# A shift filter moved from 64-channel to 32-channel diagonal blocks, in a fused convolution and token-mixing kernel

## The chip, the cores and the metric

One core of a Trainium2 chip runs the whole kernel. The metric is the device time of one execution in microseconds. Three executions before the change took 174.65, 175.32 and 174.4 us; the median is 174.65 us. The engines are named as in the profile: PE (TensorE matmul), PEld (its weight loads), DVE (VectorE), ACT (ScalarE), POOL (GpSimd) and SP (SyncE, which here only issues DMAs).

## The reference, cut to what matters

Sequence length S is 2048, channels D 448, hidden size F 1792, all in bf16.

```python
def _A_ref(q, k, v, shift_k, ssm_k, ssm_D):
    k_pad = jnp.pad(k, ((0, 0), (ks - 1, 0), (0, 0)))
    k_shift = jnp.zeros_like(k)
    for t in range(ks):                       # ks = 4
        k_shift = k_shift + k_pad[:, t:t + S, :] * shift_k[:, ks - 1 - t][None, None, :]
    kv = k_shift * v
    # y = causal convolution over S of kv with ssm_k, one filter per channel (by FFT of length 2 S)
    y = y + kv * ssm_D[None, None, :]
    return q * y

def _B_ref(x, w1, b1, w2, b2):
    h = _layernorm(x, axis=-1)
    u = _gelu(jnp.einsum("bsd,sf->bdf", h, w1) + b1)
    return (jnp.einsum("bdf,fs->bds", u, w2) + b2).transpose(0, 2, 1)

x = A_q
h = x + _A_ref(_layernorm(x, axis=-1), A_k, A_v, A_shift_k, A_ssm_k, A_ssm_D)
h2 = h + _B_ref(_layernorm(h, axis=-1), B_w1, B_b1, B_w2, B_b2)
```

The change touches the first part: the four-tap shift filter on k, its product with v, and the load of the long filter ssm_k (448 channels by 2048 positions).

## The kernel before, in words

Sequence position s is held as s = 16 q + r: q is the partition (128) and r (16 values) lies along the free axis. All SBUF tiles are views of one tensor, which the profile calls `arena`; all PSUM is `ps`, with eight banks. The stages are these, with the lines that the profile names.

- **Loads** (SP queue). The filter ssm_k comes as four chunks of channels, 128, 128, 128 and 64 (L877), the last one into 64 partitions of 4096 bytes. k comes in four pieces of four r each (L888), and so does v (L891). Small tables are the shift taps (L880, L883), ssm_D (L895) and the biases (L898, L900).
- **kT**. The filter chunks are transposed on PE (L1028) so that positions lie on partitions; DVE copies them out of PSUM (L731). Nine filler matmuls, whose result nobody reads (L1015), stand ahead of everything, and three more behind each of the first three chunks.
- **kv**. k is transposed on PE (L956) and copied out, so that channels lie on partitions. The shift filter is then a matmul with the transposed k as weights and, as the moving operand, diagonal matrices `DG` (built by DVE at L941 from an identity and the taps): a column block for each tap. A weight load holds 64 channels, so two of them, on two row tiles of 64, stand in the array side by side (L982). The work has eight units: four groups of four r, times two pairs of channel chunks. A unit fills two PSUM banks. DVE multiplies what it finds there by v and writes over v (L997, two a unit).
- **Stage 1** of the transform, for the filter ("k1") and for kv ("u1"): matmuls on four column tiles of 32 (L1049), copied out by ACT or DVE (L1059, and L1057 where ssm_D is added), and reordered across partitions by DMAs within SBUF (L1065: two on the POOL queue, one on SP, for each half group).
- **Stage 2** ("k2", "u2"): L1084, copied out by L728, L729, L731 and L732.
- **Products and first inverse stage** ("i1"): DVE products (L1150), matmuls (L1167), copies (L728), DMAs within SBUF (L1190, L1179).
- **Second inverse stage and layernorm** ("i2"): L1289 and L1297, then a chain over DVE, ACT and POOL to the normalised rows (L1375).
- **MLP**: L1422 (first seven blocks of F), L1432 (the other seven), L1444 (the second product), L1447 (residual) and the stores.

Nothing of this order is written as a loop that runs on the chip. The program hands every operation to a planner, with an estimated cost, the buffers that it reads and writes, and a due time. The due time is looked up in the table `WHEN`, by stage and step; a smaller number goes first. The planner simulates the five engines, starts on each the ready operation with the smallest number, and writes the instructions in that order, with the waits that they need. PSUM banks are given out in that simulation, singly or in pairs. Operations that may run on ACT or DVE are given to one of them by the table `WHERE` (a: ACT, d: DVE, f: whichever the planner finds free). So each engine's order is fixed when the program is built, and an instruction that waits holds back all that stand behind it on its engine.

The stage-1 matmuls read whole rows of 448 channels, so "k1" needs all four filter chunks, and "u1" needs all channels of its rows of kv.

## Time and profile before

| What | Number |
|---|---|
| median of three executions | 174.65 us |
| span of the profiled execution, first to last instruction | 173.7 us |
| PE busy | 161.4 us (93%), 1419 matmuls |
| DVE busy | 103.1 us (59%) |
| ACT busy | 89.7 us (52%) |
| POOL busy | 58.8 us (34%) |
| granted TensorE clock | 1.000 |

The median lies 0.95 us above the span of the profiled execution. The span has five stretches. Up to about 11 us the inputs arrive. From 11 to 41 us PE is busy nearly without a gap on the transposes, the shift filter and stage 1. From 41 to 73.5 us ACT and DVE are. From 73.5 to 77 us the last reorder is awaited. From 77 us to the end PE works without a gap through the second inverse stage and the MLP, 94 us of it. So what happens ahead of 77 us moves the end by as much as it moves the start of that last stretch.

### The profile page before, as it was taken

The numbers are of one execution on the slowest core, as the hardware profiler recorded it, in microseconds if no ns is written. First come the engines' busy times: TensorE is split into PE (matmuls) and PEld (weight loads), VectorE is DVE, ScalarE is ACT, GpSimd is POOL, SyncE is SP. The second block draws the span as 40 slices with busy tenths as digits, with TensorE's granted clock in tenths as the row PEclk, the third lists the DMA queues.
The fourth block names the chain that finished last, engine by engine and source line by source line (L and its number), as shares of the span: only waits on it lengthen the run. The fifth ranks groups of instructions, "written<-read, shape, count | busy, mean of one in ns | idle before, by whom it ended". The sixth has DMA issues, their size and how long they took to land.

```text
span 173.7 us, 3570 instructions
## 1 busy us (share of the span) xinstructions
PE 161.4 (93%) x1419; PEld 92.1 (53%) x1419; DVE 103.1 (59%) x191; ACT 89.7 (52%) x129; POOL 58.8 (34%) x152
## 2 busy tenths in 40 slices
PE   6989999979989999838999999999999999999994
PEld 2766745442333332424345555555567777777783
DVE  7997899868979999979897751000002132231231
ACT  3796757798999999878883455421120000000000
POOL 8345717680912524564989640000000000000000
PEclk9999999999999999999999999999999999999999
DMA  5999865783859668755999999930000111101111
GB/s 163 408 299 380 284 177 213 301 330 117 244 113 389 198 193 258 246 168 166 392 396 402 416 423 421 417 150 0 0 0 4 53 53 53 44 9 57 53 53 53
DMA packets 15628, 35.15 MB, mean 202 GB/s; under 512 B 3740, under 2 KB 9740, under 8 KB 15612
## 3 DMA queue, kind: packets, MB, share of 16 engines
q1 hardware_dynamic: 12468, 28.25, 44.7%
q0 software_dynamic: 2880, 6.49, 11.4%
q8 instruction: 11, 0.18, 0.4%
q10 hardware_dynamic: 264, 0.18, 0.3%
q14 instruction: 5, 0.04, 0.1%
HBM read 22.05 MB, written 1.84 MB: 137 GB/s over the span
## 4 chain that ended last, share of the span: by engine, by line
PE 61%; DVE 11%; DMA 10%; ACT 8%; POOL 5%; issue 2%; SPq 1%; DVEq 0%; ACTq 0%; POOLq 0%
PE ps L1444 24%; PE ps L1432 12%; PE ps L1422 9%; DMA arena<-arena 6%; DVE arena L1150 5%; DMA arena<-in_A_ssm_k_dram 5%; ACT arena L1059 4%; PE ps L1084 3%; ACT arena L728 3%; PE ps L1049 3%; PE ps L982 2%; PE ps L1167 2%; PE ps L1028 2%; DVE arena L1226 2%; ACT arena L729 2%
## 5 line engine op out<-in xcount | busy, mean ns | idle before, releaser
L1447 DVE SCALAR_TENSOR_TENSOR arena<-ps,arena 128x448 bf16<-128x448 f32 (+2 forms) x17 | 11.1, 656 | 55.7 <-PE ps L1444 55.7
L1444 PE MATMUL ps<-arena 128*128 128x448 bf16 (+2 forms) x238 | 42.7, 342 | 0.0
L1444 PEld LDWEIGHTS ps<-arena 128*128 128x128 bf16 x238 | 33.3, 145 | 9.5
L728 ACT CAST arena<-ps 128x896 bf16<-128x896 f32 (+1 forms) x31 | 24.9, 943 | 1.1 <-PE ps L925 0.6
L1422 PE MATMUL ps<-arena 128*128 128x448 bf16 x112 | 23.1, 353 | 0.9 <-DVE arena L1364 0.6
L1059 ACT CAST arena<-ps 128x896 bf16<-128x896 f32 x23 | 19.5, 913 | 6.6 <-PE ps L1049 6.5
L1065 POOL DMA_DIRECT2D arena<-arena x32 | 17.5, 553 | 13.3 <-ACT arena L1059 12.6
L1432 PE MATMUL ps<-arena 128*128 128x448 bf16 x112 | 21.7, 352 | 0.0
L1084 PE MATMUL ps<-arena 128*64 128x448 bf16 x128 | 16.0, 361 | 1.8 <-ACT arena L1059 0.9
L1412 ACT ACTIVATE arena<-ps,arena 128x448 bf16<-128x448 f32 x14 | 8.2, 640 | 17.5 <-PE ps L1432 15.1
L1150 DVE TENSOR_TENSOR arena<-arena 128x1792 bf16<-128x1792 bf16 x16 | 16.6, 1081 | 0.9 <-DMA arena<-arena 0.9
L1422 PEld LDWEIGHTS ps<-arena 128*128 128x128 bf16 x112 | 10.5, 98 | 12.2 <-DVE arena L1375 3.0
L1432 PEld LDWEIGHTS ps<-arena 128*128 128x128 bf16 x112 | 11.0, 98 | 10.2
L1167 PE MATMUL ps<-arena 64*128 64x448 bf16 x128 | 14.3, 351 | 1.8 <-DVE arena L1150 0.8
L1049 PE MATMUL ps<-arena 128*32 128x448 bf16 x256 | 15.1, 355 | 0.6 <-DVE arena L997 0.3
L1190 POOL DMA_DIRECT2D arena<-arena x14 | 8.2, 589 | 16.4 <-ACT arena L728 16.4
L1344 ACT ACTIVATE arena<-arena 128x448 bf16<-128x448 f32 x14 | 8.1, 575 | 7.1 <-DVE arena L1316 6.9
L1084 PEld LDWEIGHTS ps<-arena 128*64 128x64 f16 x128 | 5.4, 108 | 11.4 <-ACT arena L728 3.8
L1167 PEld LDWEIGHTS ps<-arena 64*128 64x128 f16 x128 | 5.0, 94 | 10.9 <-ACT arena L728 5.3
L1289 PE MATMUL ps<-arena 128*128 128x448 bf16 x32 | 7.7, 353 | 2.6 <-DMA arena<-arena 2.6
L731 DVE COPY arena<-ps 128x1024 bf16<-128x1024 bf16 (+2 forms) x15 | 9.2, 648 | 0.6 <-PE ps L1028 0.6
L1049 PEld LDWEIGHTS ps<-arena 128*32 128x32 f16 x256 | 5.0, 95 | 8.4 <-DVE arena L997 2.6
(96 smaller groups left out, 190.3 us busy)
## 6 DMA issues: line engine op xcount, KB each, us to landing
arena<-in_B_w_dram SPq DMA_DIRECT2D x8, 896.0 KB, 10.3
arena<-in_B_w_dram SPq DMA_DIRECT2D x2, 2048.0 KB, 17.5
arena<-arena SPq DMA_DIRECT2D x16, 224.0 KB, 3.4
arena<-arena POOLq DMA_DIRECT2D x32, 112.0 KB, 3.4
arena<-in_B_w_dram SPq DMA_DIRECT2D x2, 1536.0 KB, 18.9
arena<-arena POOLq DMA_DIRECT2D x14, 196.0 KB, 4.2
arena<-in_A_k_dram SPq DMA_DIRECT2D x4, 448.0 KB, 6.0
arena<-in_A_v_dram SPq DMA_DIRECT2D x4, 448.0 KB, 9.2
```

The costliest lines, as they stand in the source:

```text
L728: return e.copy(out=dst(), in_=src())
L731: return e.tensor_copy(out=dst(), in_=src())
L1049: op("pe", lambda e, W, b=b, r=r, q=q, x=x, c0=c0: e.matmul(PS[32 * q:32 * q + 32, b.slots[x], 0:D], E[:, 2 * r + x, c0:c0 + 32], src[:, r ...
L1059: return e.copy(out=dst, in_=Ppair(b)) if W == "act" else e.tensor_copy(out=dst, in_=Ppair(b))
L1065: shuf[tag].append(op(q_, lambda e, W, g=g, i=i, a=a, nu=nu, jh=jh: e.dma_start(T[a + i:a + i + 4 * nu - 3:4].rearrange("p (j k) c d -> p ...
L1084: op("pe", lambda e, W, b=bs[h], h=h, j=j, c=c, par=par: e.matmul(PS[64 * par:64 * par + 64, b.slots[c], 0:D], FW[:, 64 * c:64 * c + 64], ...
L1150: op("dve", lambda e, W, m=m, i=i: e.tensor_tensor(out=MR(m.slots[0]).rearrange("p (x y) d -> p x y d", x=2), in0=TU[:, i].unsqueeze(2).br ...
L1167: k = op("pe", lambda e, W, b=bs[h], m=ms[h], par=par, t=t, tab=tab, xy=xy, P=P: e.matmul(Pb(b, par), tab[P, :], MR(m.slots[0])[P, xy, :], ...
L1422: op("pe", lambda e, W, r=r, fc=fc, b=bs[fc]: e.matmul(Pb(b), W1A[:, r, 128 * fc:128 * fc + 128], Q[:, r, :], start=(r == 0), stop=(r == R ...
L1432: op("pe", lambda e, W, r=r, fc=fc, b=b: e.matmul(Pb(b), W1B[:, r, 128 * (fc - n0):128 * (fc - n0) + 128], Q[:, r, :], start=(r == 0), sto ...
L1444: op("pe", lambda e, W, r=r, fc=fc, b=b, d0=d0, d1=d1: e.matmul(Pb(b)[:, d0:d1], W2[fc // 7][:, fc % 7, r:S:R], G[:, fc, d0:d1], start=(fc ...
L1447: op("dve", lambda e, W, r=r, b=b, A=A, d0=d0, d1=d1: e.scalar_tensor_tensor(out=X[:, r, d0:d1], in0=Pb(b)[:, d0:d1], scalar=bm[:, r:r + 1 ...
```

## The change

Four things are changed, and the order of all instructions with them.

1. The diagonal blocks have 32 channels instead of 64. Four weight loads, on four row tiles of 32 partitions, stand in the array side by side. The units are now seven: groups of eight r for each of the three full chunks (six units), and one for the last chunk, whose two copies on the two halves of the partitions serve r 0 to 7 and r 8 to 15. A unit has 11 source rows times 4 tiles, 44 matmuls, and fills two pairs of PSUM banks, 256 columns in each bank. DVE multiplies each pair by v, 14 products of 512 elements in all. `DG` has half the columns; one small addition more builds the folded identity.
2. The filter's last chunk is loaded into all 128 partitions, with the first 1024 positions in the lower half and the others in the upper half. Its 16 transposes become 32 small ones, two for each r.
3. Behind the filter chunks one filler is left instead of nine.
4. `WHEN` and `WHERE` have new values throughout, and the planner has two new constants for DMAs.

```diff
-    "loads": (106, 111, 114, 115, 217, 195, 86, 237, 90, 235, 158, 197, 227, 143, 150,),
+    "loads": (7, 10, 12, 14, 24, 20, 2, 32, 3, 30, 19, 22, 28, 11, 16,),
...
-                        fab = s + o.nbytes / o.rate
+                        fab = s + max(190.0, o.nbytes / o.rate)
...
-        N_WZ, N_WI, N_W0, N_WK, N_WJ = 2, 0, 9, 3, 0
+        N_WZ, N_WI, N_W0, N_WK, N_WJ = 2, 0, 9, 1, 0
...
-            for i, c in enumerate((0, 1, 2, 3)):
-                sch.t0 = -20.0 + i
-                op(Dq, lambda e, W, c=c: e.dma_start(KN[0:CW[c], c, :], A_ssm_k[128 * c:128 * c + CW[c], :]),
-                   w=[(o_KN + 4096 * c, 4096)], dmab=CW[c] * 4096, rate=217.0 if c == 3 else None)
+            for c in range(3):
+                sch.t0 = -20.0 + c
+                op(Dq, lambda e, W, c=c: e.dma_start(KN[:, c, :], A_ssm_k[128 * c:128 * c + 128, :]),
+                   w=[(o_KN + 4096 * c, 4096)], dmab=128 * 4096)
+            sch.t0 = -17.0
+            op(Dq, lambda e, W: e.dma_start(
+                KN[:, 3, 0:S // 2],
+                A_ssm_k[384:448, :].rearrange("c (h s) -> h c s", h=2)),
+               w=[(o_KN + 4096 * 3, 2048)], dmab=128 * 2048)
...
-                out=DG.rearrange("p c j d -> p (c j) d"), in0=I2.unsqueeze(1).broadcast_to([128, 16, 64]),
-                in1=wsc.unsqueeze(2).broadcast_to([128, 16, 64]), op=ALU.mult),
+                out=DG.rearrange("p c j d -> p (c j) d"), in0=I2[:, 0:32].unsqueeze(1).broadcast_to([128, 16, 32]),
+                in1=wsc.unsqueeze(2).broadcast_to([128, 16, 32]), op=ALU.mult),
...
+            for u, (g, c) in enumerate(((0, 0), (0, 1), (0, 2), (0, 3), (1, 0), (1, 1), (1, 2))):
+                one = c == 3
+                bs = [_Buf(psum, 2) for _ in range(2)]
+                for m, d in enumerate((0, 4, -3, -2, -1, 1, 2, 3, 5, 6, 7)):
+                    for t in range(4):
+                        base = 8 * (t // 2) if one else 8 * g
+                        i0 = max(0, d)
+                        i1 = min(7, d + 3)
+                        P = slice(32 * t, 32 * t + 32)
+                        b = bs[t // 2]
+                        op("pe", lambda e, W, b=b, c=c, t=t, d=d, i0=i0, i1=i1, rs=rs, sh=sh, P=P, m=m: e.matmul(
+                            PS[:, b.slots[t % 2], 32 * i0:32 * i1 + 32], KX[c >> 1][P, c & 1, rs, sh:sh + 128],
+                            DG[P, c, i0 - d:i1 - d + 1, :].rearrange("p j d -> p (j d)"),
+                            start=(m == 0), stop=(m == 10), skip_group_check=True),
+                           r=[(o_KX[c >> 1] + 272 * (16 * (c & 1) + rs), 272), (o_DG, 1024)], bw=[b], n=32 * (i1 - i0 + 1),
+                           est=max(7.0, 3.4 * (i1 - i0 + 1)), mode=6)
...
-                if i < 3:
+                if i < 1:
                     dummy(N_WK, T_KT + 1.0 * (2 * i + 1), (k,))
...
-                           dmab=4 * nu * 4 * DB, keng=nu, rate=350.0))
+                           dmab=4 * nu * 4 * DB, keng=nu, rate=300.0))
```

## The prediction

> **What bounds the kernel now.** I read the page first: PE's row of slices, and the chain of work that ended last. From 77 us to the end PE has no gap, so the change can move the end only by what it moves ahead of that. The chain in order of time, the page's slices and PE's timeline then show the front.
>
> ```profile
> 2.58 8.13 DMA arena<-in_A_ssm_k_dram
> 10.76 0.96 PE ps L1028 x12
> 19.71 3.28 PE ps L982 x104
> PE   6989999979989999838999999999999999999994
> GB/s 163 408 299 380 284 177 213 301 330 117 244 113 389 198 193 258 246 168 166 392 396 402 416 423 421 417 150 0 0 0 4 53 53 53 44 9 57 53 53 53
> 1.38 3.45 PE L1015 MATMUL ps<-arena 128*128 128x448 bf16 x9 [1.38 <-DVE arena L1007]
> 10.76 0.96 PE L1028 MATMUL ps<-arena 128*128 128x128 bf16 x12 [0.62 <-DMA arena<-in_A_ssm_k_dram]
> 12.03 1.18 PE L1028 MATMUL ps<-arena 64*128 64x64 bf16 x16
> ```
>
> The chain begins with a load of the filter ssm_k: it, not PE, sets when the filter's transposes (L1028) and so its stage 1 (L1049, first at 14.00 us) begin. The second of the 40 slices (4.3 us each) moves 408 GB/s, so the loads run back to back. Then the windows, by stretch (PE, weight loads, DVE, ACT, POOL), the shift filter's own share, DVE's products, and the queues:
>
> ```profile
> 19.60:41.00 21.40, 20.03 (x404) 10.59 (x400) 18.75 (x27) 15.91 (x19) 12.00 (x23) 1.00 0.73 261
> 50.00:73.50 23.50, 21.11 (x194) 7.89 (x191) 23.12 (x36) 23.12 (x29) 8.60 (x17) 1.00 0.75 241
> 19.60:41.00 21.40, 7.16 (x208) 6.27 (x208) 1.00 0.73 261
> L997 DVE TENSOR_TENSOR arena<-ps,arena 128x512 bf16<-128x512 f32 x12 | 7.8, 684 | 0.8 <-PE ps L982 0.8
> q10 hardware_dynamic: 264, 0.18, 0.3%
> ```
>
> Between 19.6 and 41 us PE is busy 94%, but DVE 88% and ACT 74%: PE bounds, DVE stands close behind. Between 50 and 73.5 us DVE and ACT are both full.
>
> **The change part by part.** The shift filter on PE goes from 208 matmuls and 7.16 us to 7 x 44 = 308. In the trace the two row tiles of a pair start 3 to 4 ns apart, and pairs follow each other 28, 57, 82 and 110 ns apart for 64, 128, 192 and 256 columns: about 2 ns and 0.42 ns a column. A new unit has eleven sets of four tiles: five of 128 columns, two each of 96, 64 and 32, so 5 x 56 + 2 x (42 + 28 + 15) = 450 ns. Seven are 3.15 us, and with a turn of 0.02 us between units 3.3 us: 3.9 us saved. If four tiles ran only as two pairs, it would be 6.3 us and 0.9 saved; under 3 us the columns exclude.
>
> How much of it arrives: with the filter shorter, DVE is next. Its products were 12 x 0.684 + 4 x 0.414 = 9.9 us and are 14 x 0.684 = 9.6; the copies of stage 1 are still there. DVE and ACT together have 18.75 + 15.91 - 0.3 = 34.4 us, or 17.2 each if the planner shares them evenly. DVE worked at 88% in this stretch, so 17.2 / 0.88 = 19.5 us instead of 21.4: 1.9 gained. If the shares stay uneven, 18.45 / 0.88 = 21.0: 0.4. At best all 3.9 arrive. I take 1.9, the even sharing, since ACT has the room.
>
> Coarser units: the first rows of kv needed two units, four products (2.2 us of DVE); they now need four units, eight products, 8 x 0.6 = 4.8 us. So "u1" can start 2.6 us later. That is covered by the filter's stage 1, half of L1049's 256 matmuls (32 took 1.70 us, so 6.7 us), which needs no kv; without that cover it costs all 2.6. A unit also holds four of the eight PSUM banks where it held two. I take 0.5, between 0 and 2.6, nearer the covered end.
>
> The load of the last chunk. Before, it is 64 rows of 4096 bytes, issued at 3.2 us and landed 8.5 us later, at 11.7. After, the memory side is written half, channel, position: its outermost count is 2, though the SBUF side counts 128. What an outermost count does is to be seen on queue 10, which carries two DMAs alone: one of 112 rows of 896 bytes into an outer count of 8 partitions, one of 128 rows over 128. Those are 240 packets; the page has 264, and the 24 others, 4 bytes each in the packet records, are one completion for each engine used: 8 and 16. So a DMA with a side of outer count 8 ran on 8 engines, and one with a side of count 2 would run on 2. Each gets 64 pieces of 2048 bytes. Packets of 4096 bytes took 159 ns and of 3584 bytes 140 ns, so 2048 take some 82 ns: 5.2 us on these two engines, where it was 4 x 159 = 0.64. (By the page, 408 / 16 = 25.5 GB/s an engine: 131072 bytes in 5.1 us.) Ahead of it each engine has two pieces of k, 2 x 8 x 140, and three chunks, 3 x 8 x 159 ns: 6.1 us, from the first packets at 2.9. So the chunk ends at 14.2 and lands, with the 0.6 us that the first chunk took beyond its last packet, at 14.8: 3.1 later. If all 16 engines carry it, it lands up to 0.4 earlier; at worst it is the full 4.6 later.
>
> [...]
>
> Its consumers: "k1" reads whole rows, so it waits for this chunk. Before, 2.3 us went by from landing to 14.00 (16 transposes at 62 ns apart, two copies). After, 32 half-size ones, between 0.5 us if the halves overlap and 2.0 us if not; I take 1.0, half of it ahead of the first copy (0.42 us) and two hops of 0.1 us. So "k1" begins near 16.3: 2.3 us later, between 1.2 earlier (16 engines: 11.3 + 0.5 + 0.42 + 0.2, and 0.4 of other transposes, 12.8) and 3.9 later (16.3 + 1.0 + 0.42 + 0.2). All loads behind it on SP's queue end behind it on those two engines: the rest of k, the taps, and v, whose last piece moves from 19.7 to about 22.2 us. That is no more than the shift of "k1", so nothing else waits on top.
>
> Of the nine fillers behind the chunks eight go. Six of the nine (0.73 us each three) lay in the wait for the load: nothing. Three (0.54 and 0.36) stood on the chain, 0.7 us; with the load late they too would have lain in a wait, so nothing, and -0.7 if it is not late. `DG` at L941 falls from 1.22 us to about 0.65, and an addition like L939's 0.18 is added; PE is at transposes then, so nothing; without that cover -0.4. ssm_D's load is issued ahead of the third chunk, and its 0.57 us on SP delays two issues; the engines are busy with earlier chunks until 8.3, so nothing, else +0.6. The planner's constants only reorder.
>
> The new order from 41 to 73.5 us: DVE and ACT are full at 23.12 of 23.5, so it can gain 0.4; at the 88% of the stretch before it would lose 2.8. I take 0, since the work is the same. From 77 us on PE has the same matmuls without a gap: 0, and it loses what it waits for if an order fails there.
>
> Sum on the profiled execution: 173.7 + 2.3 - 1.9 + 0.5 = 174.6 us. The median stands 0.95 above that span, so 175.6 us.
>
> **The rivals.** (1) PE's saving arrives in full (3.9 instead of 1.9) and the coarser units cost nothing: 175.6 - 2.0 - 0.5 = 173.1 us, faster. It decides from the point where ACT takes over a third of what DVE copies. For it: ACT idles 5.5 of 21.4 us; against it: DVE is at 88% and alone can multiply by v. (2) The load runs on all 16 engines, as the program's planner assumes: "k1" is 1.2 earlier instead of 2.3 later, 175.6 - 3.5 = 172.1 us. For it: 128 partitions on the SBUF side; against it: the outer count of 2. (3) PE's clock falls in the wait: third chunk at about 10.7, fourth at 14.8, with one filler left, is 4 us with little work. The first nine fillers took 3.45 / 9 = 383 ns each, the later ones 190, so PE starts at half speed for some 4.6 us. Were the stage behind the wait run so for as long as those nine, 3.45 us, half of it, 1.7 us, would be lost: 177.3 us. Against it: waits of 0.62 and 2.6 us did not slow it. [...] (4) The new order leaves ACT and DVE gaps from 41 to 73.5 us as before it: up to 2.8, about 178 us.
>
> **How the numbers follow.** Load on two engines and the saving half eaten: 0.42, at 175.6, of its own 174.3 to 176.9. (1) 0.22, (2) 0.14, (3) 0.15, (4) 0.07. About 0.5% (0.87 us) is what a measurement of this kernel can tell from no change. Slower by more (over 175.5): half of the first case, 0.22, and (3) and (4), 0.44. Within: most of the rest of the first case, 0.16, and a quarter of (1), 0.22 in all. Faster: 0.34. The range from 171.7 to 177.6 leaves out the lower third of (2) and the upper ends of (3) and (4), together under 0.2.
>
> **What would show it.** Right: the last chunk lands near 15 us, with 2 completions; stage 1 begins near 16.3 us; the 308 matmuls take some 3.3 us; DVE has the fewest gaps from 20 to 41 us; the last stretch is 94 us again. Wrong: a landing near 11.5 us, filter matmuls over 5 us, PE gaps behind the products, or matmuls at half speed after 15 us.

## The result, and the profile after

| | before | after |
|---|---|---|
| median of the executions shown | 174.99 us | 187.69 us (186.17 to 189.07) |
| ratio, 95% interval | | 1.067 (1.057 to 1.077) |
| span of the profiled execution | 173.7 us | 184.8 us |
| granted TensorE clock | 1.000 | 0.972 |

The change makes the kernel 12.7 us slower. The direction of the forecast held; its size, 175.6 us, did not, and the time lies far above the range. On the profiled execution the forecast had 174.6 us and 184.8 were measured: 10.2 us are to be explained.

The lines of the page that answer to those shown of before are these: PE's slices, the granted clock, the group of the products and the queue with the two small DMAs.

```profile
PE   7935998989988998874998999999999999999994
PEclk9995799999999999998899999999999999999999
q10 hardware_dynamic: 264, 0.18, 0.3%
L1000 DVE TENSOR_TENSOR arena<-ps,arena 128x512 bf16<-128x512 f32 x14 | 9.6, 691 | 3.6 <-PE ps L986 2.1
```

The clock has two dents that before did not have, in the fourth and fifth slice and around the twentieth. The products take 9.6 us, as forecast. In the chain of waits (start, duration, what), the load of the filter that heads it is now a piece of 12.19 us, where it was 8.13, and the half-size transposes follow it:

```profile
3.68 12.19 DMA arena<-in_A_ssm_k_dram
15.91 2.13 PE ps L1032 x16
```

PE's timeline (start, duration, line, tile, form, count, and the idle time before it with what ended it) shows the two waits and what runs at half speed behind them (the last line is of before):

```profile
8.15 2.76 PE L1032 MATMUL ps<-arena 128*128 128x128 bf16 x35
15.91 2.13 PE L1032 MATMUL ps<-arena 64*64 64x64 bf16 x32 [5.00 <-DMA arena<-in_A_ssm_k_dram]
18.22 2.48 PE L963 MATMUL ps<-arena 128*128 128x128 bf16 x23
20.63 0.78 PE L1055 MATMUL ps<-arena 128*32 128x448 bf16 x8
85.79 0.79 PE L1295 MATMUL ps<-arena 128*128 128x448 bf16 x2 [3.78 <-DMA arena<-arena]
86.37 1.70 PE L1303 MATMUL ps<-arena 128*128 128x448 bf16 x4
76.98 0.55 PE L1289 MATMUL ps<-arena 128*128 128x448 bf16 x2 [2.63 <-DMA arena<-arena]
```

Stage 1 (L1055) begins at 20.63 us and the second inverse stage (L1295) at 85.79. The four matmuls of L1303 behind it took 0.92 us before. The trace's record of the granted clock has two falls to half: at 14.29 us for 6.83 us, and at 85.97 us for 3.41. The windows by stretch (PE, weight loads, DVE, ACT, POOL, clock) and the shift filter's own share (L986, PE and weight loads) are:

```profile
14.00:19.60 5.60, 3.69 (x46) 3.44 (x46) 1.14 (x3) 1.18 (x2) 0.00 (x0) 0.53 0.66 233
19.60:41.00 21.40, 19.54 (x477) 10.74 (x476) 16.03 (x22) 14.75 (x17) 10.19 (x19) 0.96 0.52 177
50.00:73.50 23.50, 21.01 (x204) 7.79 (x192) 22.49 (x28) 21.77 (x27) 10.72 (x20) 1.00 0.71 221
25.00:34.50 9.50, 5.43 (x220) 4.71 (x220) 1.00 0.70 223
39.00:42.50 3.50, 2.15 (x88) 1.93 (x88) 1.00 0.92 356
```

The filter takes 5.43 + 2.15 = 7.58 us of PE, where it took 7.16 and the forecast had 3.3. These two are busy times, in which every piece of matmuls also has the length of its last one; the forecast added up distances between starts. From first start to last in each piece, the records sum to 6.21 us before (5 pieces) and 6.14 after (8 pieces). How it runs is seen on one half of a unit, 22 matmuls of two tiles in 0.64 us, 0.46 from the first start to the last:

```profile
33.33 0.64 PE L986 MATMUL ps<-arena 32*128 32x128 bf16 x22
```

From 14 to 19.6 us DVE, ACT and POOL stand nearly still. Where the 11.1 us of the profiled executions come from is read from the first instruction of each stage:

| first instruction of | before | after | later by |
|---|---|---|---|
| stage 1 | 14.00 | 20.63 | 6.6 |
| stage 2 | 35.46 | 42.53 | 7.1 |
| first inverse stage | 51.83 | 59.96 | 8.1 |
| second inverse stage | 76.98 | 85.79 | 8.8 |
| end of the span | 173.7 | 184.8 | 11.1 |

So there are three places: 6.6 us ahead of stage 1, 2.2 us from there to the second inverse stage, and 2.3 us behind it.

The granted clock of one and the same kernel is 1.0 in some executions and 0.97 to 0.99 in others, before included; a median here holds both, so traces are compared beside medians.

### The profile page after: what moved, and what is told of

Its sections match the earlier page's. It is cut to its first block, busy times and chain, and to the rows that moved or that the text cites. A ratio compares the mean times of both kernels' runs of the same rounds, so it can differ in the third digit from the quotient of the medians.

```text
span 184.8 us, 3787 instructions
## 1 busy us (share of the span) xinstructions
PE 164.4 (89%) x1527; PEld 94.3 (51%) x1527; DVE 103.3 (56%) x188; ACT 92.7 (50%) x131; POOL 59.9 (32%) x152
## 3 DMA queue, kind: packets, MB, share of 16 engines
q1 hardware_dynamic: 12518, 28.25, 42.3%
## 4 chain that ended last, share of the span: by engine, by line
PE 64%; DVE 10%; DMA 9%; ACT 8%; POOL 5%; issue 2%; DVEq 0%; SPq 0%; POOLq 0%
PE ps L1450 23%; PE ps L1438 11%; PE ps L1428 7%; DMA arena<-in_A_ssm_k_dram 7%; PE ps L1055 6%; ACT arena L728 5%; PE ps L1173 4%; PE ps L986 3%; PE ps L1090 3%; DMA arena<-arena 3%; DVE arena L1000 3%; PE ps L1295 2%; ACT arena L1065 2%; PE ps L963 2%; PE ps L1303 1%
## 5 line engine op out<-in xcount | busy, mean ns | idle before, releaser
L1453 DVE SCALAR_TENSOR_TENSOR arena<-ps,arena 128x448 bf16<-128x448 f32 (+2 forms) x17 | 11.1, 656 | 58.1 <-PE ps L1450 58.1
L728 ACT CAST arena<-ps 128x896 bf16<-128x896 f32 (+1 forms) x30 | 24.3, 906 | 6.7 <-PE ps L930 5.3
L1428 PE MATMUL ps<-arena 128*128 128x448 bf16 x112 | 23.2, 353 | 1.0 <-DVE arena L1381 1.0
L1438 PE MATMUL ps<-arena 128*128 128x448 bf16 x112 | 22.2, 352 | 0.0
L1418 ACT ACTIVATE arena<-ps,arena 128x448 bf16<-128x448 f32 x14 | 8.9, 633 | 21.1 <-PE ps L1438 18.6
L1055 PE MATMUL ps<-arena 128*32 128x448 bf16 x256 | 16.0, 360 | 1.4 <-ACT arena L1065 0.6
L1090 PE MATMUL ps<-arena 128*64 128x448 bf16 x128 | 15.2, 359 | 1.9 <-ACT arena L728 0.6
L1438 PEld LDWEIGHTS ps<-arena 128*128 128x128 bf16 x112 | 11.0, 98 | 10.2
L1295 PE MATMUL ps<-arena 128*128 128x448 bf16 x32 | 8.4, 377 | 4.0 <-DMA arena<-arena 3.8
L1000 DVE TENSOR_TENSOR arena<-ps,arena 128x512 bf16<-128x512 f32 x14 | 9.6, 691 | 3.6 <-PE ps L986 2.1
L731 DVE COPY arena<-ps 128x1024 bf16<-128x1024 bf16 (+2 forms) x12 | 7.5, 641 | 6.8 <-PE ps L1032 4.2
L1032 PE MATMUL ps<-arena 128*128 128x128 bf16 (+1 forms) x80 | 6.1, 260 | 5.4 <-DMA arena<-in_A_ssm_k_dram 5.3
```

The source lines that it names most:

```text
L728: return e.copy(out=dst(), in_=src())
L1000: return e.tensor_tensor(out=v, in0=w_.rearrange("p t (r d) -> p t r d", d=32), in1=v, op=ALU.mult)
L1055: op("pe", lambda e, W, b=b, r=r, q=q, x=x, c0=c0: e.matmul(PS[32 * q:32 * q + 32, b.slots[x], 0:D], E[:, 2 * r + x, c0:c0 + 32], src[:, r ...
L1090: op("pe", lambda e, W, b=bs[h], h=h, j=j, c=c, par=par: e.matmul(PS[64 * par:64 * par + 64, b.slots[c], 0:D], FW[:, 64 * c:64 * c + 64], ...
L1295: k = op("pe", lambda e, W, b=b, r=r, h=h: e.matmul(Pb(b), ET[:, 2 * r + h, :], TZ[:, r, h, :], start=(h == 0), stop=(h == 1 and r >= NZ)) ...
L1428: op("pe", lambda e, W, r=r, fc=fc, b=bs[fc]: e.matmul(Pb(b), W1A[:, r, 128 * fc:128 * fc + 128], Q[:, r, :], start=(r == 0), stop=(r == R ...
```

## The experiments: the load and the wait for it

The theory was that the late chunk costs most; the rival was that the new order and the filter do. The first run keeps the order of PE, DVE, ACT and POOL as in the changed kernel and splits the load in two.

```diff
-            op(Dq, lambda e, W: e.dma_start(
-                KN[:, 3, 0:S // 2],
-                A_ssm_k[384:448, :].rearrange("c (h s) -> h c s", h=2)),
-               w=[(o_KN + 4096 * 3, 2048)], dmab=128 * 2048)
+            for h in range(2):
+                op(Dq, lambda e, W, h=h: e.dma_start(KN[64 * h:64 * h + 64, 3, 0:S // 2],
+                                                     A_ssm_k[384:448, 1024 * h:1024 * h + 1024]),
+                   w=[(o_KN + 4096 * 3, 2048, "kn3")], dmab=64 * 2048)
```

> The changed kernel with one edit: the filter's last chunk comes in two DMAs of 64 rows, one for each half of the partitions, instead of one whose memory side has an outer count of 2. Theory A (the load on two engines is late, and PE's clock falls in the wait for it): the chunk lands near 11.5 us instead of 15.9, the clock stays at full speed up to 41 us, stage 1 begins near 14.5 instead of 20.6 us, and the time falls from 187.7 by some 6 us to 180 to 183. Theory B (the new order and the coarser units cost it): the landing moves, but stage 1's gain is given back at the products, and the time stays at 185 or above.

Measured: 180.2 us, ratio 1.019 (1.005 to 1.033), 7.5 us less than the change; of its four executions two had a full clock and took 178.7 us, two a clock of 0.981 and 181.8. The two halves land at 10.90 and 11.20 us, and stage 1 begins at 15.05:

```profile
8.92 4.59 PE L1032 MATMUL ps<-arena 128*128 128x128 bf16 x67
13.67 1.45 PE L963 MATMUL ps<-arena 128*128 128x128 bf16 x23
15.05 0.56 PE L1055 MATMUL ps<-arena 128*32 128x448 bf16 x8
```

With the same data in two loads queue q1 has 12548 packets instead of 12518, 30 completions more: 16 for each load, where the one load had 2. The wait is gone: the 67 transposes, 35 of full size and 32 of half size, run in one piece. The 23 transposes of k (L963) take 1.45 us instead of 2.48, so the clock's fall behind the wait cost 1.0 us there.

The next three runs look at it from the other side. The first two put the new load and the half-size transposes into the kernel before. In the first, the program planned all engines anew.

```diff
+                A_ssm_k[384:448, :].rearrange("c (h s) -> h c s", h=2)),
...
+                        for h in (0, 1) if c == 3 else (2,):
```

> The kernel before with one part of the change: the last chunk loaded by one DMA into both partition halves, and its transposes in two halves. Order table, fillers and shift filter are those of before. Theory A: the chunk lands near 15.5 us, the clock falls in the wait, and the time rises by 4 to 7 us, to 179 to 182. Theory B: under 177.

Measured: 207.5 us, ratio 1.183 (1.168 to 1.198). It isolates nothing: the order of every engine had changed, and the clock fell five times. A table of due times fits the costs that it was made for, and a part cannot be moved into it alone. So from here on the order of every engine is held fixed. In the second, each transpose of before issues the two half-size ones, with one semaphore increment, in its place:

```diff
-                        k = op("pe", lambda e, W, ...: e.transpose(... KN[0:cw, c, r:S:R], identity=ID[0:cw, 0:cw]),
+                        def fn(e, W, ...):
+                            for P in (slice(0, 64), slice(64, 128)) if c == 3 else (slice(0, 128),):
+                                x = e.transpose(out=Pbf(b, 0)[P, ...], in_=KN[P, c, r:(S if c < 3 else S // 2):R], identity=ID[P, P])
+                            return x
```

> The kernel before, every engine's order kept instruction for instruction; only the filter's last chunk is loaded as in the change (one DMA into both halves) and transposed in 32 half-size pieces. Theory (the late chunk is the main cost): it lands near 16 us instead of 11.7, the transposes take 2.1 us instead of 1.2, the clock is at half for one or two records of 3.4 us around the wait, stage 1 begins at 20 to 21 us instead of 14.0, and the end moves by 6 to 7 us: 180 to 182 us. Rival (the wait is hidden by other work of PE and the new order is what costs): stage 1 later, but the end within 2 us of before.

Measured: 181.93 us, ratio 1.039 (1.032 to 1.046), 6.5 us above before, as the theory has it. The wait is 4.29 us, stage 1 begins at 19.91 and the second inverse stage at 83.87, 6.9 us later. The clock is at half from 17.17 us for 6.83 us, so here it falls behind the wait, and the first 32 matmuls of stage 1 take 3.18 us, where they took 1.70. Nothing hides it:

```profile
16.39 2.13 PE L1031 MATMUL ps<-arena 64*64 64x64 bf16 x32 [4.29 <-DMA arena<-in_A_ssm_k_dram]
19.91 3.18 PE L1054 MATMUL ps<-arena 128*32 128x448 bf16 x32
83.87 0.55 PE L1294 MATMUL ps<-arena 128*128 128x448 bf16 x2 [2.08 <-DMA arena<-arena]
```

The third is the changed kernel, with the order kept, and with the load and the 16 transposes of before.

```diff
+            op(Dq, lambda e, W: e.dma_start(KN[0:64, 3, :], A_ssm_k[384:448, :]),
+               w=[(o_KN + 4096 * 3, 4096)], dmab=128 * 2048)
...
+                            out=Pbf(b, 0)[:, rr * cw:rr * cw + cw], in_=KN[0:cw, c, r:S:R], identity=ID[0:cw, 0:cw]),
```

> The changed kernel, every engine's order kept; only the last chunk's load (one half, 64 rows of 4096 bytes) and its 16 transposes are those of before. Theory: the chunk lands near 11.5 us, no clock fall before 20 us, stage 1 begins near 14.0 us, the shift filter still takes 7 us on PE, the second inverse stage begins 2 us later than before's 76.98, and the time is 2 to 4 us above before: 177 to 179. Prediction's own steps without the load (saving half eaten by DVE, 0.5 for coarser units): 1.4 us below before, 173. Rival (load of little weight): 184 or more.

Measured: 180.78 us, ratio 1.029 (1.024 to 1.035). Stage 1 begins at 14.16 us and the second inverse stage at 79.13, 2.15 later than before, as expected. The end is 5.3 us later (179.0), more than the 2 to 4 expected, since the clock falls again in the wait ahead of the second inverse stage and stays at half for 6.83 us:

```profile
14.16 0.56 PE L1050 MATMUL ps<-arena 128*32 128x448 bf16 x8 [0.17 <-DVE arena L731]
79.13 0.93 PE L1290 MATMUL ps<-arena 128*128 128x448 bf16 x2 [3.78 <-DMA arena<-arena]
79.85 1.70 PE L1298 MATMUL ps<-arena 128*128 128x448 bf16 x4
```

Whether work in the wait for the chunk keeps the clock up was tried with 25 fillers in the changed kernel:

```diff
+                if i == 2:
+                    for x in range(25):
+                        op("pe", lambda e, W: e.matmul(Pb(dumb), DUM[:, 0:128], DUM, start=True, stop=True),
+                           r=[(o_DUM, DB)], bw=[dumb], n=D, after=(k,) if x == 0 else (), est=1.0)
```

> The changed kernel with 25 fillers more on PE, ahead of the last chunk's transposes; the load stays as it is. Theory A: the load lands near 15.9 us as before, but the clock does not fall between 14 and 21 us, stage 1 begins near 18 us instead of 20.6, and the time falls by 2 to 3 us, to about 185. If the clock's fall costs nothing, because the copies of DVE and ACT are what is waited for, the time stays at 187 to 188.

Measured: 187.07 us, ratio 1.065 (1.055 to 1.075): no gain. The fillers end at 15.39 us, PE still waits 0.68 us for the chunk, and the clock falls all the same, at 18.82 us, for 3.41 us. Between the fillers' end and the fall PE had, beside that wait, the 32 half-size transposes, 2.11 us, and little else. Stage 1 begins at 20.65, not near 18 as expected:

```profile
10.50 4.89 PE L1046 MATMUL ps<-arena 128*128 128x448 bf16 x25
16.19 2.11 PE L1032 MATMUL ps<-arena 64*64 64x64 bf16 x32 [0.68 <-DMA arena<-in_A_ssm_k_dram]
```

It also shows that the transposes cost 2.11 us at full clock as well, 66 ns each: the two halves do not overlap.

## The experiments: the shift filter

In the changed kernel's trace the filter runs two tiles at a time. All but one of its seven units were written as 22 matmuls of tiles 0 and 1 and then 22 of tiles 2 and 3, since each half takes its banks by itself and the planner may start it alone. So its matmuls follow each other at the distances of pairs, 22 ns a matmul on average; only the last ten matmuls of the one unit written in fours stand 34 ns apart. The first try had a unit take both bank pairs at once, on top of the run with two loads:

```diff
-                           ... bw=[b], n=32 * (i1 - i0 + 1),
+                           ... bw=bs if m + t == 0 else [b], n=32 * (i1 - i0 + 1),
```

> The two-load version of the changed kernel, in which a unit's first matmul takes both pairs of banks, so that the planner can place the four row tiles in turn, where it placed all of two tiles ahead of the other two. If four tiles run together, a unit's 44 matmuls take 0.45 to 0.5 us instead of 0.98, 3.5 us of PE less in all, and the time falls by 1 to 3 us against the two-load version. If the array runs only two at a time, a unit stays at 0.95 to 1.0 us.

Measured: 200.94 us, ratio 1.145 (1.132 to 1.157). This too was planned anew and isolates nothing. Next, the changed kernel with the old load was taken, and only the 44 matmuls of each unit were put in fours, after planning: in the order of the source rows, to the place of the 23rd of them, while all else keeps its order.

```diff
         order = self.schedule()
+        key = {i: (x, 0) for x, i in enumerate(order)}
+        for u in self.units:
+            late = max(key[i] for i in u)
+            first = sorted(key[i][0] for i in u)[len(u) // 2]
+            for x, i in enumerate(u):
+                key[i] = (first, x)
...
```

> As the run with the old load, and the 44 matmuls of every shift-filter unit are put in the order of the source rows, four tiles in turn, where the planner had put 22 of two tiles ahead of 22 of the two others; the order of all else is kept. If four tiles run at the pitch that the prediction took for them: 0.47 us a unit, 3.3 in all instead of 7. Rival (PE's supply of instructions limits: in the trace of after the last matmuls of the one unit that was emitted in fours follow each other 34 ns apart): 0.65 to 0.75 us a unit, 5 in all. The time against the old-load run: up to 2 to 3.5 us less if PE bounds from 19 to 41 us; within 0.5 us if DVE's products and the banks bound there.

Measured: 185.51 us, ratio 1.061 (1.053 to 1.069), 4.7 us slower than the same kernel with pairs. A unit took 0.58 to 0.65 us from its first start to its last, waits left out, where the clock was full; the forecast's pitch gives 0.47. And PE waited for the products to free banks (waits of PE from 14 to 50 us: total, times, longest):

```profile
PE ps L1012 <- DVE arena L1027: 4.6, 4, 1.5
```

That leaves two questions: what a unit costs PE, and how much of the 2.2 us is the new order's. For the second, the new filter alone was put into before's order, with each engine's list given to the program as numbers; four units stand in the places of the first four old ones, three in the next three.

```diff
+FORCED = {
+    "pe": (
+        (1, 9), (128, 12), (119, 8), (150, 12), (141, 8), (516, 8), (507, 4), (525, 3), (511, 4), (537, 8),
...
+                    if forced[e]:
+                        x = forced[e][-1]
+                        if npred[x] == 0 and not started[x] and ready_t[x] <= t + 1e-6 and can_acquire(ops[x]):
+                            cand = x
+                            forced[e].pop()
```

> The kernel before with the new shift filter alone: the load, the transposes and the fillers of before, and before's order of every engine held fixed, the first four of the seven new units in the places of the first four of the eight old ones, the other three in the next three places; within a unit 22 matmuls of two tiles, then 22 of the two others, as in the changed kernel. Theory (the filter's gain was never there, and what was left of the loss with the old load, 2.2 us by the second inverse stage, comes from the new order): the filter takes 7 us, the second inverse stage begins within 1 us of 76.98, and the time is within 1 us of before. Rival (the coarser units cost it): the second inverse stage 2 us later, 176.5 to 177. The prediction's step, if order and supply let it: 1.4 to 1.9 us below before.

Measured: 177.67 us, ratio 1.012 (0.994 to 1.029). The theory in this expectation fell. From stage 1 (13.63 us) to the second inverse stage (78.96) it is 65.3 us; before it was 63.0, and in the changed order with the old load 65.0. The two sums are nearly the same, but not their parts. Counted from stage 1, the first instructions of stage 2, of the first and of the second inverse stage come 2.9, 2.7 and 2.3 us later than before in this run, and 0.25, 1.3 and 2.0 later in the changed order. So before's order loses it at the filter and the changed order mostly behind it, and equal sums do not show one cause. The filter takes 8.98 us, more than before's 7.16, and the first four units run at 5.49 / 176 = 31 ns a matmul, the last 1.5 us of them at half clock, which falls at 23.24 us for 3.41. On PE's timeline they are one piece:

```profile
19.27 5.49 PE L1066 MATMUL ps<-arena 32*128 32x128 bf16 x176
```

The filter's own windows (length, PE, weight loads, clock, DMA share, GB/s) stand here for three kernels, in three fences: this one, then the two below with one increment for two matmuls and with one for four.

```profile
19.20:36.00 16.80, 8.98 (x308) 8.12 (x308) 0.90 0.57 197
```

```profile
19.20:36.00 16.80, 7.23 (x308) 6.38 (x308) 1.00 0.63 218
```

```profile
19.20:36.00 16.80, 4.50 (x308) 3.77 (x308) 1.00 0.58 202
```

With the matmuls in fours in this order (a pair in the list is a first number and a count; the 44 of a unit now go in a row):

```diff
-        (549, 8), (172, 12), (185, 2), (189, 2), (193, 2), (197, 2), (201, 2), (205, 2), (209, 2), (213, 2),
...
+        (549, 8), (172, 12), (185, 44), (231, 44), (277, 44), (323, 44), (630, 8), (588, 2), (836, 8), (590, 6),
```

> The same with the 44 matmuls of a unit in fours. By the supply limit seen in the row of matmuls at the end of a kernel (41 queued at the tiles' pitch, then 34 ns each): 0.5 us for a unit that follows a wait, 0.6 to 0.8 for others, 5 us in all. A unit needs four free banks at its start, so PE waits for DVE's products as in the run with fours in the changed order (4.6 us there). Theory: the waits take the gain, and it is 1 to 5 us slower than with pairs. Rival (that was the changed order's doing): faster than with pairs by up to 2 us.

Measured: 182.36 us, ratio 1.037 (1.022 to 1.051), the second inverse stage at 83.30, 4.3 us behind the pairs: the waits again, as expected.

What a unit costs PE was measured by itself: rows of 132 matmuls behind the last product of the kernel before, which lengthen it by what they take.

```diff
+            for rows, tiles, cols in ((32, 4, 128), (32, 4, 32), (32, 2, 128), (32, 2, 32), (64, 2, 128)):
+                for y in range(132 // tiles):
+                    for t in range(tiles):
+                        ...  # one matmul, weights of its own, tile t
```

> The kernel before with five rows of 132 matmuls behind its last product, each with its own weight load of 128 columns: four tiles of 32 rows in turn with 128 and with 32 columns, two tiles of 32 rows with 128 and 32, two tiles of 64 rows with 128. By the prediction's pitch: 14, 7, 28, 14 and 28 ns a matmul. By a supply limit of 34 ns for each weight load and matmul, once what was queued is used up: 34 ns in all five.

Measured, in the starts of the records: the first 41 matmuls of the first row follow the tiles' pitch, four within 11 ns and the next four some 55 ns after the first, so 14 ns each, as the prediction had it. From the 42nd on they start one by one, 34 ns apart, to the end of the row. Four tiles with 32 columns: 34 ns for all 132. Two tiles with 32 columns: 14 at first, then 34. From 178.79 us the clock was at half, and the pairs of 128 columns there follow each other by 107 ns. In the windows of this trace, 40 matmuls touch half a microsecond at first, then 71 touch 2.2 us:

```profile
171.70:172.20 0.50, 0.50 (x40) 0.50 (x41) 1.00 0.00 0
173.00:175.20 2.20, 2.20 (x71) 2.20 (x67) 1.00 0.16 37
```

The limit is there, but that could be PE's supply of instructions or the semaphore increment that every matmul of this kernel makes. The next run repeats the rows with fewer increments:

```diff
+            for cols, per in ((128, 1), (128, 4), (32, 1), (32, 4), (128, 44), (32, 44)):
+                        def fn(e, W, ...):
+                            for q in range(per):
+                                k = e.matmul(...)
+                            return k     # only this one increments the semaphore
```

> As the run with rows of matmuls behind the kernel's end: six rows of 132 matmuls on four tiles of 32 rows in turn, 128 or 32 columns, each with its own weight load. In rows 1 and 3 every matmul increments the semaphore when it is done, as all of this kernel's do; in rows 2 and 4 every fourth does, in rows 5 and 6 every 44th. Theory (PE's supply of instructions limits): 34 ns a matmul in all six once the queue is used up. Rival (the semaphore increments follow each other 34 ns apart): rows 2, 4, 5 and 6 at the tiles' pitch, 14 ns a matmul at 128 columns (28 at half clock) and 7 to 9 at 32 (14 at half clock).

Measured: the rival is right. At 128 columns it is 34 ns a matmul with an increment each. In the row with one in four, the first 31 are still 34 ns apart, behind the row ahead; from then on it is 14.8 ns to the end of the row. At 32 columns with one in four, starts are 9, 8, 8 and 34 ns apart in turn, so the step of 34 ns goes with the increment. With one in 44 it is 26.7 ns at 128 columns and some 9 at 32. (From 180.56 us on this trace is at half clock.) The four later rows each have a pause of 0.5 to 1.4 us, whose cause was not sought. The windows of the two rows show it, 82 matmuls in 2.60 us against 124 in 2.30:

```profile
171.00:173.60 2.60, 2.60 (x82) 2.60 (x79) 1.00 0.19 50
173.80:176.10 2.30, 2.30 (x124) 2.30 (x121) 1.00 0.03 7
```

So with an increment each the rows settle at 34 ns a matmul, the first of them once some 41 small matmuls are through; with fewer increments they keep the tiles' pitch, 14.8 ns at 128 columns. Then the repair, in the kernel itself and in before's order, with one increment for each pair of matmuls:

```diff
+                    for h in range(2):
+                        def fm(e, W, ...):
+                            for t in range(2 * h, 2 * h + 2):
+                                x = e.matmul(...)
+                            return x
+                        op("pe", fm, ..., bw=[bs[h]], ...)
```

> As the run with the new filter in before's order with pairs, but each pair of matmuls makes one semaphore increment instead of two. By the increments, 34 ns each: the first four units take 3.7 us instead of 5.49, the filter 6.4 instead of 9.3, the second inverse stage begins 2 to 2.9 us earlier than 78.96, and the time is at most that of before, 173 to 175. Rival (DVE's products and the banks take it up): 176 or more.

Measured: the first row of the three windows above turns into the second, 8.98 to 7.23 us; from stage 1 (14.02) to the second inverse stage (77.51) it is 63.5 us, 1.8 less than with an increment each and 0.5 more than before. Not all of the 1.8 is the increments, since that run had a fall of the clock amid the filter and this one had none there. The last run of this document, with the same filter, 12 fillers and a fall at 22.44 us, needs 64.7 for it, so like with like the increments are some 0.6 and the fall some 1.2. The first four units end 4.57 us after their start, 0.85 of it a wait: their 3.7 us are as expected, the filter's 6.4 are not. The time is 177.4 us, ratio 1.007 (1.002 to 1.012), above the 175 expected: in nine of ten executions the clock was at 0.99 or lower, in the profiled one by a fall at 78.69 us. Then one increment for four, in fours:

```diff
+                    for h in range(1):
+                            for t in range(4 * h, 4 * h + 4):
+                        op("pe", fm, ..., bw=bs, ...)
```

> The new filter in before's order in fours, one increment for four matmuls. By the increments and the tiles' pitch: 0.48 us a unit, 3.4 in all, the prediction's figure. But a unit still needs four free banks at its start, so PE waits for the products between units: with fours and an increment each, the run was 4.4 us behind the pairs by the second inverse stage. Theory: PE's time is no longer the limit, the waits are, and it stays 3 us or more slower than pairs with one increment. Rival: the filter's gain arrives, 173.

Measured: 178.53 us, ratio 1.020 (1.014 to 1.026). Now each unit takes 0.47 us from its first start to its last, the prediction's own figure, 3.3 us for seven; with the last matmul's length it is the 4.50 us of the third window. But PE waits for banks ahead of the units, 3.8 us in all, held by ACT's and DVE's copies of stage 1 and by the products:

```profile
PE ps L1055 <- ACT arena L1132: 1.8, 4, 0.7
PE ps L1055 <- DVE arena L1071: 1.3, 2, 0.8
PE ps L1055 <- DVE arena L1130: 0.7, 1, 0.7
```

The second inverse stage begins at 79.50, 2.0 us later than with pairs. The theory held in its direction; the 3 us were 2.0 in the trace, and 1.1 by the medians.

## The experiments: fillers and the clock

Eight of the nine fillers behind the chunks, cut from 448 to 8 columns in the kernel before, places kept:

```diff
+                N = 8 if after and (i, len(small_f)) != (0, 0) else D
+                op("pe", lambda e, W, N=N: e.matmul(Pb(dumb)[:, 0:N], DUM[:, 0:128], DUM[:, 0:N], start=True, stop=True),
```

> The kernel before with eight of the nine fillers behind the filter's chunks cut from 448 to 8 columns, everything in its place. Prediction's step: the time is the same within 0.5 us, or 0.7 less if those on the chain count. Rival: with less work in the waits for the chunks the clock falls before 20 us, and it is 1.7 to 3.4 us slower.

Measured: 176.17 us, ratio 1.001 (0.997 to 1.006). In the trace stage 1 begins 0.7 us earlier (13.32) and the second inverse stage 1.2 earlier (75.75), and then the clock falls at 76.43 us for 3.41. Nine of ten executions had a clock of 0.99 or less, against five of thirteen of before on the same chip.

Then 18 fillers in the wait ahead of the second inverse stage, in the changed kernel with the old load:

```diff
+                    for x in range(18 if r == 0 else 0):
+                        op("pe", lambda e, W, b=b: e.matmul(Pb(b), FW, view(o_DR, [D], f16), start=True, stop=True),
+                           r=r_fw + [(o_DR, DB)], bw=[b], n=D, est=1.0, safter=ct_last if x == 0 else ())
```

> As the run with the old load (changed kernel, last chunk loaded and transposed as before), and 18 fillers of 448 columns stand on PE in the wait ahead of the second inverse stage, 3.4 us of the 3.78. Theory (the rest of the loss is half clock after that wait, 2.8 us in the trace, and 2.2 us of later arrival): the clock does not fall near 78 us, the stage still begins near 79.2 us, and the time is 2 to 3 us below the old-load run's 180.8: 178. Rival (the clock falls whatever stands in the wait, or the fillers delay the stage): 180 or more.

Measured: 179.92 us, ratio 1.026 (1.020 to 1.031). In the profiled execution the clock stays at full speed, the stage begins at 79.32 us and the span is 176.6, 2.4 less than without the fillers, as the theory has it. The medians differ by only 0.9: of the five executions three had a clock of 0.99 all the same, and one with a full clock took 179.9 too. Where the clock fell there was not seen. The same with 12 fillers in the kernel before:

```diff
+                    for x in range(12 if r == 0 else 0):
```

> The kernel before with 12 such fillers in its wait of 2.63 us ahead of the second inverse stage. In some executions of the kernel before the mean clock is 0.990 and the span 1.3 to 2 us longer. Theory (that is one record of half clock set off by this wait): all executions at a clock of 0.998 or more, and the median up to 1 us lower. Rival (set off elsewhere): the same spread as before.

Measured: 174.78 us, ratio 0.995 (0.991 to 0.999), the clock at 0.998 or more in all ten executions, where before had 0.99 in most. The theory holds. This is the fastest kernel of the case that is told from before by its interval, by half a per cent. With the fillers behind the chunks cut as well:

```diff
+                N = 8 if after and (i, len(small_f)) != (0, 0) else D
...
+                    for x in range(10 if r == 0 else 0):
```

> The kernel before with eight fillers behind the chunks cut to 8 columns and 10 fillers in the wait ahead of the second inverse stage. Theory: the chain is shorter by 0.7 us at stage 1 and 1.2 at the second inverse stage, as in the trace of the run with the eight cut, and the clock stays up: 173.5, 1 us below before. Rival (a fall of the clock earlier in the span eats it): as before.

Measured: 174.55 us, ratio 0.998 (0.993 to 1.003). The second inverse stage begins at 76.11, and the span is 172.6; but four of ten executions have a clock of 0.99 or less, so both the theory and its rival are partly right. Last, the filter with one increment a pair, with 12 fillers:

```diff
+                        op("pe", fm, ..., bw=[bs[h]], ...)
...
+                    for x in range(12 if r == 0 else 0):
```

> The pairs with one increment, and 12 fillers in the wait ahead of the second inverse stage. Theory: as that run, without its executions at a clock of 0.99: 173 to 174.5, at or below the kernel before with the same fillers (174.8). Rival: 176.

Measured: 176.43 us, ratio 1.004 (0.999 to 1.009). The theory's 174.5 was missed; the profiled execution has a fall at 22.44 us, amid the filter. The repaired filter is no gain over before.

## Why the prediction was wrong, step by step

Three terms of the sum failed. The late chunk was to put stage 1 off by 2.3 us and put it off by 6.6. The filter, with its units, was to give 1.4 us by the second inverse stage, and 2.2 were lost. The last stretch was to stay as it was, and grew by 2.3.

**The load: right, a little short.** Two engines, as argued: the chunk's semaphore counts two completions, at 15.81 and 15.87 us, and in the packet records 128 packets of 2048 bytes start two by two from 8.79 to 14.93 us. The forecast had 9.0 and 14.2. A packet took 6.14 us / 64 = 96 ns instead of 82, and the landing came 0.9 us behind the last one's end instead of 0.6: 15.9 instead of 14.8, 4.2 us later than before. That completions follow the outer count queue 10 had shown for a destination alone, 8 with an outer count of 8; this load shows it for a source, 2 with an outer count of 2. The upper bound of 4.6 covered it; rival (2) is excluded.

**The consumers: mis-sized.** The 32 transposes took 2.13 us, where 1.0 was taken between bounds of 0.5 and 2.0; the two halves follow each other. Half of that was put ahead of the first copy, and nothing else. In the trace 23 transposes of k stand behind the waiting instruction on PE, with no wait of their own, and come ahead of stage 1. With the old load they were done in time for stage 1 at 14.16, so all that is queued behind the late chunk slips by as much as the chunk. From landing to stage 1 it was 4.7 us, not 1.5.

**Rival (3), the clock in the wait: it happened, twice.** It had 0.15 and 1.7 us; against it stood that before's waits of 0.62 and 2.6 us did not slow PE. The wait was 5.00 us, and the forecast's own landing already made it 4. In the trace PE's last work before the wait ended at 10.9 us and the clock fell at 14.29, 3.4 us later. It cost 1.0 us in the transposes of k and some tenths around them. The step that lacked was to price the wait that the first step had just made. The second fall was in no rival: the wait ahead of the second inverse stage grew from 2.63 to 3.78 us, and the last stretch, forecast as "94 us again", lost 2.3 us, of which half of 3.41 us, 1.7, is the clock. With the clock kept up it was 0.6 longer than before (176.6 - 79.32 = 97.3 us against 96.7).

**PE's saving: there was none.** Set pitches of 56, 42, 28 and 15 ns gave 3.3 us for 308 matmuls, on the assumption that four tiles run side by side. The changed kernel's program writes them two at a time, but for one unit, so its filter takes 6.14 us between starts, close to the forecast's own lower case of 6.3. That case was to save 0.9 all the same, since the forecast set distances between starts against a busy time, 7.16; between starts, before took 6.21. So the lower case saves nothing, and four tiles at the full pitch would have saved 2.9 and not 3.9. The full pitch is real (0.467 us a unit, forecast 0.45 to 0.47), but only where fewer matmuls increment a semaphore. With one increment each, the pace is 34 ns once some 41 matmuls are through; in the changed kernel that slowed ten matmuls, in before's order the first four units. The trace before could not tell that limit from columns: a pair's widths add up to 444 ns for 14 matmuls, 31.7 ns each. And at the full pitch, in before's order, the gain still does not arrive, because four banks a unit are not free in time.

**What of it reaches the end, and the coarser units.** The 1.9 gained and the 0.5 lost became 2.2 lost by the second inverse stage. The even sharing did not come: from stage 1 to stage 2, with the old load, DVE was busy 17.30 and ACT 15.38 us of 21.7, where it was 19.20 and 15.42 of 21.5. In before's order, of 2.3 us lost with the new units 0.6 went with the increments, 1.2 with a fall of the clock, and 0.5 is left to the units. That half microsecond is the forecast's own figure, but there it stands net of PE's time and beside a gain that did not come, so it is no proof of that step.

**Fillers, `DG`, ssm_D's load.** The fillers' "nothing" held in time, and so did the 0.7 us on the chain if the load is not late: the trace has it, and the clock's falls took it back. The products took 9.6 us as worked out. `DG` and ssm_D's load show nothing on the chain.

**The order from 41 to 73.5 us: 0 is not borne out, and rival (4) is not excluded.** Counted from stage 1, and with the old load, the changed order's last stage-2 matmul starts 1.3 us earlier than before's, but the last of the first inverse stage 1.5 later, and the second inverse stage 2.0. In the chain, the last reorder ahead of that stage took 4.51 us before and takes 5.18 in the changed kernel:

```profile
72.42 4.51 DMA arena<-arena
80.57 5.18 DMA arena<-arena
```

So part of the 2.2 us comes behind the filter and may be the order's; the changed order with the old filter was not run, and how much is the order's and how much the units' stays open. The changed order also brought the longer last wait, and with it the second fall: in before's order with the new units that wait is 2.0 to 2.3 us.

The three places of the loss, then: 4.2 us landing, 1.0 transposes and about 1.4 for the clock and what is queued (6.6); 2.2 for the units and the order together; 1.7 for the second fall and 0.6 left unexplained. Together 11.1.

## What to carry to other kernels

When a step of the forecast makes a wait, carry the wait on: list what is queued behind it on its engine, and ask what the clock does in it and for how long after. Before pricing many small matmuls by their columns, read in which order the program writes them, count their semaphore increments, and price the buffers that they hold until they are read. Set distances between starts against distances between starts, not against busy time. A plan made by a table of due times fits one set of costs; a part is tested by holding every other order fixed, not by letting the program plan anew.

## What the runs showed of the hardware that was not expected

- Rows of small matmuls with a semaphore increment each settled at 34 ns a matmul, at 128 columns and at 32. Four tiles of 32 rows at 128 columns ran at 14.8 ns a matmul with one increment in four, and the first 41 of a row ran at the tiles' pitch even with one each.
- In two traces the clock's falls lie on a grid of 3.413 us: in the changed kernel at 14.29 and 85.97 us, 21 steps apart; in the first, newly planned run with the late load at 14.93, 38.82, 52.47, 76.37 and 103.67, which is 7, 4, 7 and 8 steps. Of the eight falls whose length is given here seven last 3.41 or 6.83 us, and one 17.07. The kernel before has both cases: it waits 2.63 us ahead of the second inverse stage, keeps a full clock in some executions and shows 0.99 in others, and with 12 fillers in that wait the clock stayed at 0.998 or more in all ten. That such a wait costs something or nothing by where it falls on that grid is the author's estimate from these falls; no run tested it.
- The clock also falls while PE is busy. In the rows of matmuls it fell at 178.79 us, after a step of four tiles of 32 rows with 32 columns at 34 ns each, and stayed at half for 17.07 us; with the new units in before's order it fell at 23.24 us amid the filter; and in the changed kernel with 25 fillers it fell at 18.82 us, behind a wait of 0.68 us and 2.11 us of 64 by 64 transposes. What sets it off there stays open; with one increment a pair the filter ran once without a fall and once with one. The two windows are of the rows of matmuls, ahead of the fall and behind it:

```profile
175.40:178.70 3.30, 3.30 (x103) 3.30 (x99) 0.00 (x0) 0.00 (x0) 0.00 (x0) 1.00 0.02 5
178.80:195.80 17.00, 17.00 (x398) 16.96 (x397) 0.00 (x0) 0.00 (x0) 0.00 (x0) 0.50 0.01 3
```
